# A transformer block on one core: chunks of 256/512/512/512/256 tokens, paired PSUM banks dealt by the scheduler, a separate home for parked sums, and the softmax's maximum taken and subtracted in PSUM

## The chip, the cores and the metric

The kernel runs on one core of a Trainium2 chip. The metric is the device time of one execution in microseconds (us). All executions compared here are in the fast state; of all runs of this study one (of the halved-evictions experiment) fell in the slow state, and it is left out of its verdict.

The engines are called PE (TensorE, matmuls), PEld (its weight loads), DVE (VectorE), ACT (ScalarE), POOL (GpSimd) and SP (SyncE, which issues most transfers). Each engine works through its own queue in the order in which the kernel emits its instructions (the run with statistics on ACT, below, shows what that can cost: DVE waits 6.32 us for an eviction that stands behind other work), so that order is part of the design. "Bank" is one of the 8 parts, each 512 fp32 columns wide, into which the kernel divides PSUM; the matrix unit's results land there, and ACT or DVE carries them out ("eviction").

## The reference, cut to what matters

```python
# x: 2048 tokens x 512, bf16; 32 heads of 16; F = 1792
mod = silu(c) @ w_mod                      # six vectors of 512: sa, ca, ga, sb, cb, gb
h = layernorm(x) * (1 + ca) + sa           # first layernorm, affine from c
q, k, v = split(h @ wqkv)                  # 1536 columns
logits = einsum(q, k at s, s-2, ..., s-14) / 4     # 8 keys per query, 2 apart
attn = softmax(logits)                     # over those 8
x = x + ga * ((attn . v at s, s-2, ...) @ wo)
h = layernorm(x) * (1 + cb) + sb           # second
h = layernorm(h)                           # third
u = gelu(h^T @ w1 + b1)                    # mixes over the 2048 tokens: 512 x 1792
x = x + gb * (u @ w2 + b2)^T
```

The first MLP product sums over tokens. It can therefore be computed in levels: a level adds the tokens that are ready, and the sums are "parked" in between.

## The kernel before

The kernel builds a list of operations with their dependences and estimated durations, and a small list scheduler in Python fixes the order per engine (and, where an operation may run on ACT or DVE, the engine). It works on 4 chunks of 512 tokens. The parts that matter:

```python
# PSUM: fixed roles for the 8 banks
psA = [psp.tile([P, 512], F32, name=f"psA{i}") for i in range(2)]
psL = psp.tile([P, 2, 512], F32, name="psL")          # logits, 8 windows x 128
psT, psX, psO, psW = ...                              # one bank each
# home of the projection weights, later of the parked sums (same memory)
w_raw = wg[:, 0:KT * 3 * D]...;  gT = wg[:]...
...
# start: w_mod through ACT's queue (1 MB), wqkv in one load (1.5 MB);
# columns sa and 1+ca by 32 one-column matmuls; then
#   bqkv = sa @ wqkv                       (48 one-column matmuls, PE)
#   w_raw *= (1 + ca)                      (4 operations, DVE)
...
# softmax of a chunk, after the logits lie in psL
copy2(lsb[b], psL, ...)                               # eviction
m4 = max(lsb[0:4], lsb[4:8]); m2 = ...; m1 = ...      # DVE
lsb = lsb - m1                                        # DVE
ee = exp(lsb)                                         # ACT
s4 = ee[0:4] + ee[4:8]; s2 = ...; s1 = ...            # DVE
rb = reciprocal(s1); ee = ee * rb                     # DVE
...
# layernorm statistics: bn_stats + bn_aggr on DVE, or two summing
# activations and three small ones on ACT, as the scheduler picks
# second MLP product: 16 tiles of 128 tokens, banks psA[0], psA[1] in turn
```

Of the kernel before, what the change touches and what calls it, by code (L numbers as in the profile page):

```python
# [13 lines left out]
P = 128  # L14
# [9 lines left out]
class _Op:  # L24
    __slots__ = ("idx", "alts", "eng", "dur", "lat", "fn", "name", "deps", "succ", "start", "end", "bytes_", "pk")
# [7 lines left out]

class _Graph:
    XLAT = 0.3
    EBIAS = {}
# [3 lines left out]
    def __init__(self):  # L40
        self.ops = []
        self.last_writer = {}
        self.readers = {}
        self.pk = 0.0

    def add(self, eng, dur, fn, reads=(), writes=(), name="", lat=0.0, after=(), bytes_=0, pk=None):
        return self.add_any([(eng, dur, fn)], reads, writes, name, lat, after, bytes_, pk)

    def add_any(self, alts, reads=(), writes=(), name="", lat=0.0, after=(), bytes_=0, pk=None):
        op = _Op(len(self.ops), list(alts), lat, name, bytes_, self.pk if pk is None else pk)  # L50
        deps = set(a.idx for a in after if a is not None)
        for k in reads:
            w = self.last_writer.get(k)
            if w is not None:
                deps.add(w)
        for k in writes:
            w = self.last_writer.get(k)
            if w is not None:
                deps.add(w)
            deps.update(self.readers.get(k, ()))  # L60
        for k in reads:
            self.readers.setdefault(k, []).append(op.idx)
        for k in writes:
            self.last_writer[k] = op.idx
            self.readers[k] = []
        deps.discard(op.idx)
        op.deps = deps
        self.ops.append(op)
        return op

    def schedule(self):
# [7 lines left out]
        avail = set(o.idx for o in ops if not o.deps)  # L79
        order = []  # L80

        def ready_time(o, e):
            r = 0.0
            for d in o.deps:
                od = ops[d]
                t = od.end + (0.0 if od.eng == e else self.XLAT)
                if t > r:
                    r = t
            return r

        while avail:
            per_eng = {}
            for i in avail:
                o = ops[i]
                fin = [(max(ready_time(o, e), eng_free.get(e, 0.0)) + d, e, d) for (e, d, _) in o.alts]
                best_fin = min(f_ + self.EBIAS.get(e, 0.0) for f_, e, d in fin)
                for f_, e, d in fin:
                    if f_ + self.EBIAS.get(e, 0.0) <= best_fin + 0.05:
# [13 lines left out]
            o.start = r  # L112
            if o.bytes_:
# [3 lines left out]
            else:  # L117
                o.end = r + o.dur + o.lat
            eng_free[e] = r + o.dur
# [53 lines left out]
def _t_tt2(n):  # L173
    return 0.15 + 0.00051 * n
# [6 lines left out]
def _t_ts(n):  # L181
    return 0.12 + 0.00043 * n


def _t_act(n, aps=0):
    return 0.12 + 0.00095 * n + 0.06 * aps
# [7 lines left out]
def kernel(  # L194
# [13 lines left out]
    C: int = 512,  # L208
    ORDER: int = 1,
    DUMP: int = 0,  # L210
    RK=(10, 20, 30, 40, 50),
    MK: int = 1000,
    WIN: int = 25,
    LEVELS=(2, 3),
    PARK: int = 0,
    FLEX: int = 1,
    DBIAS: int = 100,
    XLAT: int = 30,
):
    nc = _OrderedNC(tc, ORDER)  # L220
    G = _Graph()
    G.WIN = WIN / 100.0
    G.EBIAS = {"dve": DBIAS / 100.0}
    G.XLAT = XLAT / 100.0
    SB = C // 4
    NCH = S // C
    TPC = C // P
    WPM = min(NW, 512 // SB)
    NHALF = NW // WPM

    x_flat = A_x[0]
    out_flat = out[0]
    x_view = x_flat.rearrange("(t p) d -> p t d", p=P)
    w1_view = B_w1.rearrange("(t p) f -> p t f", p=P)
    w2_view = B_w2.rearrange("(t p) s -> p t s", p=P)
    wmod_view = w_mod.rearrange("(kt p) n -> p kt n", p=P)
    wo_view = A_wo.rearrange("(h q l) n -> l h q n", h=H, q=4, l=4)
# [7 lines left out]
    psA = [psp.tile([P, 512], F32, name=f"psA{i}") for i in range(2)]  # L245
    psL = psp.tile([P, 2, 512], F32, name="psL")
    psT = psp.tile([P, 512], F32, name="psT")
    psX = psp.tile([P, 512], F32, name="psX")
    psO = psp.tile([P, 512], F32, name="psO")
    psW = psp.tile([P, 512], F32, name="psW")  # L250
    psM = [psT, psX, psO]
    NA = 2
    ctrA = [0]

    def nextA():
        ctrA[0] += 1
        return (ctrA[0] - 1) % NA

    xx = T([P, NST, D], BF, "xx")
    wg = T([P, NFT * D], BF, "wg")  # L260
    w_raw = wg[:, 0:KT * 3 * D].rearrange("p (k n) -> p k n", k=KT)
    gT = wg[:].rearrange("p (f d) -> p f d", f=NFT)
    woq = T([P, 4, D], BF, "woq")
    h3 = T([P, NST, D], BF, "h3")
    NB2 = 2
    n_sb = [T([P, TPC, D], BF, "n_sb0")] * NB2
    hT = [T([P, KT, C], BF, f"hT{i}") for i in range(NB2)]
    q_sb = [T([P, 4, C], BF, f"q_sb{i}") for i in range(NB2)]
    k_c = [T([P, 4, PAD + C], BF, f"k_c{i}") for i in range(NB2)]
    v_c = [T([P, 4, PAD + C], BF, f"v_c{i}") for i in range(NB2)]  # L270
    NPROD = 2
    prod = [T([P, 4, NW, SB], BF, f"prod{i}") for i in range(NPROD)]
    lsb = [T([P, NW, SB], BF, f"lsb{i}") for i in range(NB2)]
    ee = [T([P, NW, SB], BF, f"ee{i}") for i in range(NB2)]
    a2sb = [T([P, 2, C], BF, f"a2sb{i}") for i in range(NB2)]
    m4 = T([P, 4, SB], BF, "m4")
    m2 = T([P, 2, SB], BF, "m2")
    m1 = T([P, SB], BF, "m1")
    s4 = T([P, 4, SB], BF, "s4")
    s2 = T([P, 2, SB], F32, "s2")  # L280
    s1 = T([P, SB], F32, "s1")
    rb = T([P, SB], BF, "rb")
    NVD = 3
    vD = [T([P, 8, C + 8], BF, f"vD{i}") for i in range(NVD)]
    NPV = 4
    pv = [T([P, 4, C], BF, f"pv{i}") for i in range(NPV)]
    o_sb = [T([P, 4, C], BF, f"o_sb{i}") for i in range(NB2)]
    h2 = [T([P, TPC, D], BF, f"h2{i}") for i in range(NB2)]
    junk = T([P, D], BF, "junk")
    NWS = 3  # L290
    wst = [T([P, NFT, 256], BF, f"wst{i}") for i in range(NWS)]
    ostage = [h2[i][:].rearrange("p a d -> p (a d)")[:, 2 * D:3 * D] for i in range(2)]
    otmp = [h2[i][:].rearrange("p a d -> p (a d)")[:, 0:2 * D].bitcast(F32) for i in range(2)]
# [7 lines left out]
    sac_bf = T([P, KT], BF, "sac_bf")  # L301
    bqkv = T([P, 12], F32, "bqkv")
# [12 lines left out]
    st6 = [T([P, TPC, 6], F32, f"st6_{i}") for i in range(2)]  # L315
    mv = [T([P, TPC, 2], F32, f"mv{i}") for i in range(2)]
    lv1 = [T([P, TPC], F32, f"lv1_{i}") for i in range(2)]
    rs1 = [T([P, TPC], F32, f"rs1_{i}") for i in range(2)]
    sums = [T([P, TPC, 2], F32, f"sums{i}") for i in range(2)]
    sums1 = [T([P, TPC, 2], F32, f"sums1_{i}") for i in range(2)]  # L320
    sums3 = [T([P, TPC, 2], F32, f"sums3_{i}") for i in range(2)]
    nb1 = [T([P, TPC], F32, f"nb1_{i}") for i in range(2)]
    st6b = [T([P, TPC, 6], F32, f"st6b_{i}") for i in range(2)]
    mv2 = [T([P, TPC, 2], F32, f"mv2_{i}") for i in range(2)]
    lv2 = [T([P, TPC], F32, f"lv2_{i}") for i in range(2)]
    rs2 = [T([P, TPC], F32, f"rs2_{i}") for i in range(2)]
    nb2 = [T([P, TPC], F32, f"nb2_{i}") for i in range(2)]
    st6c = [T([P, TPC, 6], F32, f"st6c_{i}") for i in range(2)]
    mv3 = [T([P, TPC, 2], F32, f"mv3_{i}") for i in range(2)]
    lv3 = [T([P, TPC], F32, f"lv3_{i}") for i in range(2)]  # L330
    rs3 = [T([P, TPC], F32, f"rs3_{i}") for i in range(2)]
    nb3 = [T([P, TPC], F32, f"nb3_{i}") for i in range(2)]
# [3 lines left out]
    def copy2(dst, src_fn, n, bf16_src, reads, writes, name, scale=None):  # L336
        def fa():
            if scale is None:
                nc.scalar.activation(dst, src_fn(), ACT.Identity)
            else:  # L340
                nc.scalar.activation(dst, src_fn(), ACT.Identity, scale=scale)

        def fd():
            if scale is None:
                nc.vector.tensor_copy(dst, src_fn())
            else:
                nc.vector.tensor_scalar(dst, src_fn(), scale, None, op0=ALU.mult)
        alts = [("act", _t_act(n), fa)]
        if FLEX:
            alts.append(("dve", (0.12 + 0.00052 * n) if bf16_src else _t_tt1(n), fd))  # L350
        return G.add_any(alts, reads=reads, writes=writes, name=name)

    def dma(out_ap, in_ap, nbytes, reads, writes, name):
        return add("sp", 0.65, lambda: nc.sync.dma_start(out_ap, in_ap), reads=reads, writes=writes, name=name,
                   bytes_=nbytes)

    def ln_stats(src_fn, evac_dst, st6_ap, mv_ap, sums_ap, reads, writes, name):
        def fd():
            x = src_fn()
            if evac_dst is not None:  # L360
                nc.vector.tensor_copy(evac_dst, x)
                x = evac_dst
            nc.vector.bn_stats(st6_ap, x)
# [504 lines left out]
```

## Time and profile before

The kernel before took 254.2 us (median of 3 runs, 253.66 to 254.49); the profiled execution had a span of 251.4 us.

| Stretch (us) | What happens | What limits it |
|---|---|---|
| 0 to 17.6 | loads, first layernorm, columns from c, weight scaling | waits on loads |
| 20 to 120 | most of the attention of the four chunks | DVE |
| 147 to 194 | most of the first MLP product | PE |
| 198.7 to 247.2 | second MLP product, 16 groups of 14 matmuls | PE |
| 247.2 to 251.4 | last eviction and store | tail |

First, lines of the page of the kernel before: the busy time of each engine with its share of the span, then the span in 40 equal slices, each digit the busy share in tenths; "PEclk" is the granted TensorE clock in tenths.

```profile
span 251.4 us, 3545 instructions
...
PE 209.5 (83%) x1295; PEld 91.2 (36%) x1295; DVE 166.0 (66%) x238; ACT 152.3 (61%) x343; POOL 7.8 (3%) x32
...
PE   0188994998989236996789989999899999999993
...
DVE  3169999899999998799955998214900044444443
...
PEclk9999997799999755697999999999999999999999
...
```

PE is busy most of the time, but not all: in the 14th and 15th slice (a slice is 6.3 us, so 82 to 94 us) its row drops to 2 and 3 while the DVE row stays at 9, and the clock row falls with it. The next lines are from the table of busy time by windows of the kernel before (window, its length, then each engine's busy time with the number of its instructions, the granted clock, the share and rate of the transfers).

```profile
...
core 0: us, PE busy (x) PEld busy (x) DVE busy (x) ACT busy (x) POOL busy (x), PEclk, DMA share, GB/s
20.00:40.00 20.00, 16.45 (x103) 7.22 (x102) 19.19 (x30) 14.48 (x32) 1.49 (x9) 1.00 0.42 112
40.00:60.00 20.00, 18.11 (x136) 7.24 (x135) 18.91 (x19) 14.75 (x24) 1.90 (x2) 0.83 0.82 134
60.00:80.00 20.00, 18.69 (x151) 8.29 (x151) 19.63 (x22) 16.04 (x36) 0.67 (x1) 1.00 0.68 105
80.00:100.00 20.00, 9.24 (x60) 2.89 (x59) 19.29 (x33) 17.60 (x42) 0.89 (x1) 0.62 0.66 90
100.00:120.00 20.00, 17.36 (x116) 7.21 (x116) 17.05 (x18) 15.81 (x39) 0.00 (x0) 0.78 0.14 18
...
```

DVE is busy 19.19, 18.91, 19.63 and 19.29 of 20 us up to 100 us, PE only 9.24 of 20 in the last of them. DVE is the bottleneck of this stage. PE stands idle for 10.8 us of the last window; the list of its waits puts about half of that down to DVE (5.3 us) and half to ACT (5.6 us), mostly to ACT's late evictions of the one bank psO. The start is read from the timeline of PE in the kernel before (start, duration, operation, and in brackets the idle time before it with what ended it):

```profile
...
2.21 0.18 PE L144 MATMUL psT<-ident,c_t 4*128 4x4 bf16 x1 [2.21 <-DMA c_t<-in_c_dram]
11.79 0.40 PE L144 MATMUL psO<-ident,b_t 14*128 14x14 bf16 x2 [9.39 <-DMA b_t<-in_B_b_dram]
12.12 1.01 PE L144 MATMUL psX<-sc,vD_96 128*128 128x1 bf16 x32
...
17.63 2.33 PE L144 MATMUL psA_61<-hT_73,wg 128*128 128x512 bf16 x4
...
```

PE idles 9.39 us and the profile puts the wait down to a bias load. Finally, the softmax on DVE, from the groups of instructions of the kernel before (operation, tiles, shapes, count, then busy time in us, mean ns of one, and the idle time before):

```profile
...
L144 DVE RECIPROCAL rb<-s_94 128x128 bf16<-128x128 f32 x4 | 3.8, 952 | 0.1
...
L144 DVE TENSOR_TENSOR lsb_84<-lsb_84,m_91 128x1024 bf16<-128x1024 bf16 x2 | 1.4, 693 | 0.1
L144 DVE TENSOR_TENSOR ee_85<-ee_85,rb 128x1024 bf16<-128x1024 bf16 x2 | 1.4, 692 | 0.1
...
L144 DVE TENSOR_TENSOR m_89<-lsb_84 128x512 bf16<-128x512 bf16 x2 | 0.8, 418 | 2.8 <-ACT lsb_84 L144 2.8
...
```

One reciprocal of 128 columns costs 952 ns, the subtraction and the scaling 692 ns each. The first step of the maximum tree had waited 2.8 us for ACT to copy the logits out of PSUM.

### The profile page before, as it was taken

Reading aid. Unit: us, or ns where it says so; the run is one execution under the profiler, and the core shown is the slowest. Engines: PE = TensorE matmul, PEld = TensorE weight load, DVE = VectorE, ACT = ScalarE, POOL = GpSimd, SP = SyncE. Lnnn points to the kernel's source line nnn. Section 1 sums busy time; section 2 is a strip of 40 time slices with the busy share of each in tenths; the row PEclk is TensorE's granted clock in tenths of the full one; section 3 lists DMA queues with packets and bytes.
Section 4 is the critical chain, followed back from the end, with each engine's and each line's share of the span. In section 5 each row is a group of like instructions: output and inputs, shape, how many; then the busy total and the mean of one; then the engine's idle time right before and its main releaser. Section 6 shows DMA issues by size and latency. Waiting matters only on the chain.

```text
span 251.4 us, 3545 instructions
## 1 busy us (share of the span) xinstructions
PE 209.5 (83%) x1295; PEld 91.2 (36%) x1295; DVE 166.0 (66%) x238; ACT 152.3 (61%) x343; POOL 7.8 (3%) x32
## 2 busy tenths in 40 slices
PE   0188994998989236996789989999899999999993
PEld 0163431433434002432234433444344344444441
DVE  3169999899999998799955998214900044444443
ACT  5178568768886889697997797688786400000000
POOL 4000110011001100000000000000000000000000
PEclk9999997799999755697999999999999999999999
DMA  6995239974880099300009994123424966666311
GB/s 244 385 296 165 83 124 146 149 174 85 147 110 3 0 157 141 45 0 1 0 25 170 151 247 128 43 71 95 128 87 122 319 190 202 206 196 207 104 42 42
DMA packets 46596, 32.87 MB, mean 131 GB/s; under 512 B 2036, under 2 KB 45556, under 8 KB 46580
## 3 DMA queue, kind: packets, MB, share of 16 engines
q1 hardware_dynamic: 45984, 31.60, 53.9%
q10 hardware_dynamic: 596, 1.06, 1.1%
q8 instruction: 10, 0.16, 0.3%
q14 instruction: 6, 0.05, 0.1%
HBM read 22.03 MB, written 2.10 MB: 96 GB/s over the span
## 4 chain that ended last, share of the span: by engine, by line
PE 52%; DVE 18%; ACT 16%; DMA 8%; issue 3%; SPq 2%; ACTq 0%; DVEq 0%
PE psA_61 L144 19%; PE psA_62 L144 19%; PE psW L144 5%; PE psT L144 4%; DMA wst_108<-in_B_w_dram 4%; DMA b_t<-in_B_b_dram 4%; ACT junk L144 3%; DVE h_106 L144 3%; ACT h_71 L144 2%; PE psL L144 2%; ACT h_106 L144 2%; PE psO L144 2%; SPq L144 2%; DVE st6c_158 L144 1%; DVE rb L144 1%
## 5 line engine op out<-in xcount | busy, mean ns | idle before, releaser
L144 PEld LDWEIGHTS <-wg 128*128 128x128 bf16 x240 | 22.9, 118 | 34.1 <-issue 18.8
L144 DVE SCALAR_TENSOR_TENSOR h_105<-psA_61,b2col,gb_bc 128x512 f32<-128x512 f32 x8 | 6.0, 751 | 30.0 <-PE psA_61 L144 30.0
L144 PEld LDWEIGHTS <-wst_108 128*128 128x128 bf16 x164 | 15.9, 98 | 21.3 <-DMA wst_108<-in_B_w_dram 2.4
L144 PEld LDWEIGHTS <-wst_109 128*128 128x128 bf16 x156 | 15.0, 98 | 19.9 <-issue 2.2
L144 PE MATMUL psA_61<-hT_74,wg 128*128 128x512 bf16 x48 | 15.0, 437 | 3.8 <-DVE k_c_78 L144 1.9
L144 PEld LDWEIGHTS <-wst_110 128*128 128x128 bf16 x128 | 12.4, 98 | 15.3 <-issue 0.4
L144 PE MATMUL psA_62<-hT_74,wg 128*128 128x512 bf16 x48 | 14.0, 419 | 2.5 <-ACT q_sb_76 L144 1.5
L144 ACT ACTIVATE junk<-xx 128x512 bf16<-128x512 bf16 x23 | 14.5, 629 | 0.6
L144 PE MATMUL psA_61<-hT_73,wg 128*128 128x512 bf16 x48 | 13.7, 401 | 1.1 <-ACT k_c_77 L144 1.0
L144 DVE SCALAR_TENSOR_TENSOR h_106<-psA_62,b2col,gb_bc 128x512 f32<-128x512 f32 x8 | 6.0, 751 | 12.4 <-PE psA_62 L144 12.4
L144 ACT ACTIVATE xx<-psW 128x512 bf16<-128x512 f32 x15 | 9.0, 598 | 6.9 <-PE psW L144 6.7
L144 PE MATMUL psA_62<-hT_73,wg 128*128 128x512 bf16 x48 | 12.5, 384 | 0.0
L144 PE MATMUL psW<-woq,o_sb_104 128*128 128x512 bf16 x32 | 10.7, 461 | 0.3 <-ACT o_sb_104 L144 0.3
L144 PE MATMUL psA_61<-h_71,wst_108 128*128 128x512 bf16 x40 | 9.8, 379 | 0.8 <-DMA wst_108<-in_B_w_dram 0.8
L144 DVE CAST wg<-psA_61 128x512 bf16<-128x512 f32 x4 | 2.8, 692 | 11.5 <-PE psA_61 L144 11.4
L144 PE MATMUL psO<-pv_101,stack_113 128*32 128x512 bf16 x32 | 3.6, 443 | 8.0 <-ACT o_sb_104 L144 4.6
L144 PE MATMUL psA_61<-wg,wst_108 128*128 128x512 bf16 x42 | 9.6, 379 | 0.6 <-DMA wst_108<-in_B_w_dram 0.6
L144 PE MATMUL psT<-ident,n_sb_72 128*128 128x128 bf16 x64 | 6.8, 265 | 3.8 <-ACT hT_74 L144 2.5
L144 PE MATMUL psA_62<-h_71,wst_108 128*128 128x512 bf16 x40 | 9.8, 379 | 0.0
L144 DVE TENSOR_TENSOR prod_81<-q_sb_76,k_c_78 128x4096 bf16<-128x4096 bf16 x4 | 9.2, 2288 | 0.9 <-ACT q_sb_76 L144 0.9
L144 PE MATMUL psA_62<-wg,wst_108 128*128 128x512 bf16 x42 | 9.6, 379 | 0.0
L144 PE MATMUL psA_61<-wg,wst_109 128*128 128x512 bf16 x42 | 9.6, 379 | 0.0
(211 smaller groups left out, 442.5 us busy)
## 6 DMA issues: line engine op xcount, KB each, us to landing
wst_108<-in_B_w_dram SPq DMA_DIRECT2D x3, 896.0 KB, 4.8
wst_109<-in_B_w_dram SPq DMA_DIRECT2D x3, 896.0 KB, 4.8
vD_97<-v_c_79 SPq DMA_DIRECT2D x16, 130.0 KB, 5.5
vD_96<-v_c_80 SPq DMA_DIRECT2D x16, 130.0 KB, 4.5
xx<-in_A_x_dram SPq DMA_DIRECT2D x4, 512.0 KB, 10.9
wst_110<-in_B_w_dram SPq DMA_DIRECT2D x2, 896.0 KB
wg<-in_A_wqkv_dram SPq DMA_DIRECT2D x1, 1536.0 KB, 9.4
wst_108<-in_B_w_dram SPq DMA_DIRECT2D x3, 512.0 KB, 6.3
```

The costliest lines, as they stand in the source:

```text
L144: r = fn(*a, **k)
```

## The change

Its intent: take work off DVE and off the start, let PE start MLP work as soon as tokens are ready, and use the PSUM banks more freely. The diff, cut to its core (`...` marks cuts; the scheduler's cost figures and its bookkeeping of banks are left out):

```diff
-    C: int = 512, ...  LEVELS=(2, 3),
+    SIZES=(2, 4, 4, 4, 2),  LEVELS=(2, 3, 4),     # in tiles of 128 tokens
...
-    psA = [... for i in range(2)];  psT, psX, psO, psW = one bank each
+    psG = [psp.tile([P, 1024], F32, name=f"psG{i}") for i in range(3)]
+    def ps(slot):                 # slot.i is picked by the scheduler
+        lo = slot.i % 2 * 512
+        return psG[slot.i // 2][:, lo:lo + slot.size * 512]
...
-    w_raw = wg[:, 0:KT * 3 * D]...;  gT = wg[:]...
+    w_raw_t = T([P, KT * 3 * D], BF, "w_raw")     # later a home for w2
+    gT = T([P, NFT, D], BF, "gT")
...
+    # x of the first chunk in two tiles, w_mod in two parts, w_raw in three
+    for t in (1, 0, 2): dma(w_raw[:, :, t*D:(t+1)*D], ...)
-    bqkv = sa @ wqkv;  w_raw *= (1 + ca)
+    # the affine rides on the eviction of the transposes
+    nc.vector.tensor_scalar(hT[:, kt, :], src(), a1col, sacol, mult, add)  # or ACT
...
-    lsb = copy(psL); m4, m2, m1 = max tree; lsb -= m1; ee = exp(lsb)
-    s4, s2, s1 = sum tree; rb = reciprocal(s1); ee *= rb
+    nc.vector.tensor_reduce(m1, psL, XY, max)                   # DVE, from PSUM
+    matmul(psL, lhsT=-identity, rhs=m1, start=False)            # PE subtracts
+    nc.scalar.activation(ee, psL, Exp, scale=DH ** -0.5)        # ACT, from PSUM
+    for w in range(8): matmul(ps(s_s), lhsT=identity, rhs=ee[:, w])   # PE sums
+    rb = exp(-ln(sum))                                          # ACT
+    ee *= rb                                                    # DVE, as before
...
-    layernorm statistics on DVE or ACT, as the scheduler picks
+    layernorm statistics on DVE (but for two tiles of the second
+    layernorm in chunks 2 to 4, which ACT sums while evicting)
...
-    evictions of 512 columns
+    evictions of 1024 columns, two banks at a time, where a pair is free
+    # the last tile of the second MLP product in two halves of 256 columns
```

## The prediction

> **What bounds it now.** The page: span 251.4 us (time 254.2, 2.8 us more); PE busy 83%, DVE 66%, ACT 61%. By stretches (busy table over windows):
> - 0 to 17.6 us, start: PE idles 9.4 us for the bias loads (waits), because a bias matmul stands first in PE's order. First projection matmul at 17.6 us, steady from 22 us.
> - 20 to 120 us, attention: DVE is busy 90 to 100% in most 10 us windows. PE depends on it: 4.7 and 4.5 of 10 us busy in 80 to 100, granted clock 0.75 and 0.50 there.
> - 147 to 194 us, first MLP product, and 198.7 to 247.2, second: PE saturated. The second is 16 groups of 14 matmuls at 3.02 us (chain of waits), 216 ns each. The Trainium skill (TensorE: Matmul & The Clock Gate, Back-to-back issue gap) gives 512/2.4 + 2.5 = 216 ns; the trace agrees.
> - Tail 4.2 us.
>
> **What changes.**
> - Start: bias loads leave PE's way; two 128 KB x tiles and split weight loads come first; scaling the projection weight (2.2 us DVE), its bias product (1.8 us PE) and the 9.4 us wait go, the affine rides on the transposes' eviction. Projections should start near 9 us: about -9.
> - DVE: softmax max, subtract and sum trees plus reciprocal (about 4 us a chunk, times 4) become a max reduce from PSUM, about 1.2 us by estimate (the skill, VectorE: DVE Perf Modes, Side-by-side, counts one element a cycle; the 692 ns of a 512-wide PSUM copy fits). But all first and third and part of the second layernorm statistics go to DVE: 42 pairs of 0.80 us against 25. Summing the instruction list with the trace's durations, DVE before the final stage stays about 139 us (143 before).
> - ACT: pairs of banks halve the evictions (1.01 us for 1024 columns against 2 x 0.59); statistics leave. Sum about 132 us against 152.
> - PE: +14 parking reads (3.0 us), +negated-max products (2) and exp sums (2.5), -bias products. Sum about 201 us, 5 more.
> - Own parking home, more homes for the second weights: PE idled only 0.6 us there, so little. Halved last tile: about -1.
>
> **Critical path.** In PE's new order no MLP matmul stands before the fourth chunk's logits. DVE has 84.5 us of work up to there. With 5 us done by 14 us, the rest at 93% busy (20 to 120 us of before: 93%) ends near 99 us. From there PE has about 126 us: 106 MLP, 20 attention remainder. DVE needs 54 us more, which the MLP covers. So 99 + 126, + 3 stalls, + 3 tail, + 2.8 = 234; I shade it to 231 since ACT is lighter and may let DVE reach 95%.
>
> **Prediction: 231 us, range 222 to 241; faster by over 2%: 0.95, within 2%: 0.03, slower: 0.02.**
>
> **Right if** the profile shows the first projection matmul by 10 us, DVE at or above 93% from 14 to 99 us, the first MLP matmul at 95 to 103 us, PE idle under 4 us from there to the last matmul, second product again 48.4 us, DVE before the final stage 135 to 143 us, ACT 125 to 140.
>
> **Wrong if** six paired banks make PE wait on ACT evictions in attention; the PSUM reduce or the 4096-wide product over overlapping reads is slower than assumed; the serial chain max, subtract, exp, sum, log, exp stalls DVE; PE loses clock before 99 us; or DVE's idle gaps vanish (under 222).

## The result

The changed kernel took 238.31 us (median of 4 runs, 238.14 to 238.81) beside 253.93 us (251.75 to 254.49, 4 runs) for the kernel before. The ratio is 0.942, with a 95% interval from 0.937 to 0.947. Ratios, here and below, are worked out from the fast runs of both kernels in the same rounds, and so are not quite the ratio of the medians quoted. It is 15.6 us faster. The output was correct.

The same rows of the page of the changed kernel:

```profile
span 236.5 us, 3678 instructions
...
PE 206.4 (87%) x1413; PEld 100.6 (43%) x1436; DVE 157.8 (67%) x231; ACT 129.4 (55%) x209; POOL 3.7 (2%) x29
...
PE   0493678899988995889999999999999999999992
...
DVE  4207979997999979989969987662600044444445
...
PEclk9999599999999999999999999999999999999998
...
```

and its table by windows:

```profile
...
core 0: us, PE busy (x) PEld busy (x) DVE busy (x) ACT busy (x) POOL busy (x), PEclk, DMA share, GB/s
20.00:40.00 20.00, 12.64 (x106) 6.75 (x108) 17.61 (x38) 12.34 (x23) 0.00 (x0) 0.83 0.63 182
40.00:60.00 20.00, 19.00 (x146) 9.00 (x147) 18.69 (x23) 13.45 (x22) 0.00 (x0) 1.00 0.65 141
60.00:80.00 20.00, 17.67 (x157) 8.31 (x159) 19.81 (x18) 17.63 (x27) 0.00 (x0) 1.00 0.83 118
80.00:100.00 20.00, 17.12 (x130) 9.53 (x131) 18.36 (x26) 16.09 (x32) 0.00 (x0) 1.00 0.35 63
100.00:120.00 20.00, 18.58 (x184) 8.91 (x186) 17.69 (x13) 14.16 (x23) 0.00 (x0) 1.00 0.75 164
...
```

In 80 to 100 us PE is now busy 17.12 of 20 us instead of 9.24, at a granted clock of 1.00 instead of 0.62. DVE is still busy 18.36 there, so it still sets the pace, but each chunk needs less of it. Over the whole kernel DVE's busy time fell from 166.0 to 157.8 us and ACT's from 152.3 to 129.4. The start, in the timeline of PE in the changed kernel:

```profile
...
10.55 0.37 PE L188 MATMUL psG_63<-hT_71,w_raw 128*128 128x256 bf16 x1 [2.20 <-DMA w_raw<-in_A_wqkv_dram]
11.96 3.39 PE L188 MATMUL psG_63<-hT_71,w_raw 128*128 128x256 bf16 x15 [1.04 <-DMA w_raw<-in_A_wqkv_dram]
15.14 2.67 PE L188 MATMUL psG_61<-hT_71,w_raw 128*128 128x256 bf16 x16
17.65 1.91 PE L188 MATMUL psG_62<-hT_71,w_raw 128*128 128x256 bf16 x16
...
```

The first projection matmul starts at 10.55 us instead of 17.63, but the next one waits again for the weight load, and the 15 matmuls after that take 3.39 us where the 16 of the group at 17.65 take 1.91 us. DVE in the same stretch of the changed kernel:

```profile
...
9.31 0.73 DVE L188 TENSOR_SCALAR hT_71<-psG_62,a1col,sacol 128x256 bf16<-128x256 bf16 x2 [0.69 <-ACT hT_71 L188]
18.96 1.23 DVE L188 TENSOR_TENSOR big_78<-q_sb_72,k_c_74 128x2048 bf16<-128x2048 bf16 x1 [8.93 <-issue]
20.10 0.69 DVE L188 BATCH_NORM_STATS2 st_0_1_123<-xx 128x6 f32<-128x512 bf16 x1
...
23.31 1.19 DVE L188 TENSOR_TENSOR big_79<-q_sb_72,k_c_74 128x2048 bf16<-128x2048 bf16 x1
...
```

DVE gets its first query-key product ("big" from q and k) at 18.96 us, after 8.93 us of idling. The profile calls the cause "issue", but ACT's eviction of q ends at 18.87 us in the same trace, just ahead of it. Behind that first product DVE runs the four statistics pairs of the second chunk, from 20.10 us to the product at 23.31 us; while DVE stood idle these lay behind the product in its queue. Where the PE-bound part begins, in PE's timeline of the changed kernel:

```profile
...
104.21 1.02 PE L188 MATMUL psG_61<-h_69,wst_98 128*128 128x512 bf16 x3 [1.00 <-ACT a2sb_83 L188]
...
```

The first matmul of the MLP ("h" times "wst") comes at 104.21 us. From there to PE's last matmul, which ends at 232.2 us, PE is busy 126.7 of 128.0 us. In the kernel before, the first MLP matmul came at 130.35 us, and from there to the last PE was busy 114.4 of 116.8 us. So the MLP starts 26.1 us earlier, and 11.2 us of that are given back because PE has more work left at that point; the difference, 14.9 us, is that of the two profiled spans. The new maximum, from the groups of the changed kernel:

```profile
...
L188 DVE TENSOR_REDUCE m_87<-psL 128x128 bf16<-128x1024 f32 x3 | 3.6, 1212 | 0.8 <-PE psL L188 0.8
...
```

And the end, in the timeline of DVE in the changed kernel:

```profile
...
226.19 0.75 DVE L188 SCALAR_TENSOR_TENSOR o_sb_95<-psG_62,b2col,gb_bc 128x512 f32<-128x512 f32 x1 [3.18 <-PE psG_62 L188]
...
227.58 0.74 DVE L188 SCALAR_TENSOR_TENSOR o_sb_95<-psG_62,b2col,gb_bc 128x512 f32<-128x512 f32 x1
...
230.74 0.75 DVE L188 SCALAR_TENSOR_TENSOR o_sb_95<-psG_61,b2col,gb_bc 128x512 f32<-128x512 f32 x1 [1.69 <-PE psG_61 L188]
...
```

The evictions of the second product come in twos: one waits 3.18 us for PE, the next follows at once. In the kernel before, there was one per 3.02 us, each after a wait of 1.54 us, as in this line of its DVE timeline:

```profile
...
241.19 0.75 DVE L144 SCALAR_TENSOR_TENSOR h_106<-psA_62,b2col,gb_bc 128x512 f32<-128x512 f32 x1 [1.54 <-PE psA_62 L144]
...
```

The tail after the last matmul is 4.3 us in the changed kernel and was 4.2.

### The profile page after: what moved, and what is told of

Read it like the earlier page. It is cut to its first block, busy times and chain, and to the rows that moved or that the text cites. A ratio compares the mean times of both kernels' runs of the same rounds, so it can differ in the third digit from the quotient of the medians.

```text
span 236.5 us, 3678 instructions
## 1 busy us (share of the span) xinstructions
PE 206.4 (87%) x1413; PEld 100.6 (43%) x1436; DVE 157.8 (67%) x231; ACT 129.4 (55%) x209; POOL 3.7 (2%) x29
## 4 chain that ended last, share of the span: by engine, by line
PE 58%; DVE 17%; ACT 11%; issue 7%; DMA 4%; SPq 1%; DVEq 0%; ACTq 0%
PE psG_61 L188 21%; PE psG_62 L188 21%; PE psG_63 L188 15%; ACT xx L188 3%; DMA w_raw<-in_A_wqkv_dram 3%; DVE big_78 L188 2%; DVE big_79 L188 2%; DVE st_0_1_123 L188 2%; DVE big_80 L188 2%; ACT junk L188 2%; ACT h_69 L188 2%; PE psL L188 1%; DMA vD_93<-v_c_77 1%; SPq L188 1%; DVE st_2_1_143 L188 1%
## 5 line engine op out<-in xcount | busy, mean ns | idle before, releaser
L188 PEld LDWEIGHTS <-w_raw 128*128 128x128 bf16 x282 | 30.8, 114 | 28.1 <-issue 7.6
L188 DVE SCALAR_TENSOR_TENSOR o_sb_95<-psG_62,b2col,gb_bc 128x512 f32<-128x512 f32 x6 | 4.5, 748 | 24.6 <-PE psG_62 L188 24.6
L188 PEld LDWEIGHTS <-wst_99 128*128 128x128 bf16 x128 | 12.2, 98 | 15.6 <-issue 1.8
L188 PE MATMUL psG_61<-hT_71,w_raw 128*128 128x512 bf16 (+1 forms) x78 | 17.8, 372 | 0.9 <-DVE ga_bc L188 0.5
L188 PE MATMUL psG_62<-hT_71,w_raw 128*128 128x256 bf16 (+1 forms) x95 | 17.7, 327 | 0.5 <-ACT hT_71 L188 0.4
L188 PE MATMUL psG_63<-hT_71,w_raw 128*128 128x256 bf16 (+1 forms) x62 | 13.0, 360 | 3.3 <-DMA w_raw<-in_A_wqkv_dram 3.2
L188 DVE TENSOR_TENSOR big_78<-q_sb_72,k_c_74 128x2048 bf16<-128x2048 bf16 (+1 forms) x5 | 8.2, 1646 | 8.9 <-issue 8.9
L188 PEld LDWEIGHTS <-ident 128*128 128x128 bf16 (+1 forms) x99 | 7.9, 97 | 12.4 <-issue 5.6
L188 DVE TENSOR_TENSOR n_sb<-o_sb_95,xx 128x512 bf16<-128x512 f32 (+1 forms) x17 | 11.2, 660 | 0.6
L188 PE MATMUL psG_62<-h_69,wst_99 128*128 128x512 bf16 x40 | 10.8, 379 | 0.5 <-issue 0.3
L188 ACT ACTIVATE gT<-psG_62 128x1024 bf16<-128x1024 f32 x9 | 9.2, 1017 | 3.4 <-PE psG_62 L188 3.4
L188 PE MATMUL psG_63<-h_69,wst_99 128*128 128x512 bf16 x39 | 10.7, 380 | 0.1
L188 DVE SCALAR_TENSOR_TENSOR o_sb_95<-psG_61,b2col,gb_bc 128x512 f32<-128x512 f32 (+1 forms) x6 | 4.2, 703 | 8.0 <-PE psG_61 L188 8.0
L188 PE MATMUL psG_62<-h_69,wst_100 128*128 128x512 bf16 x35 | 8.9, 380 | 0.1
L188 ACT ACTIVATE gT<-psG_63 128x1024 bf16<-128x1024 f32 x7 | 7.1, 1016 | 2.7 <-PE psG_63 L188 2.7
L188 DVE SCALAR_TENSOR_TENSOR o_sb_95<-psG_63,b2col,gb_bc 128x512 f32<-128x512 f32 (+1 forms) x5 | 3.5, 693 | 6.3 <-PE psG_63 L188 6.3
## 6 DMA issues: line engine op xcount, KB each, us to landing
out_dram<-n_sb SPq DMA_DIRECT2D x15, 128.0 KB, 1.7
```

The costliest lines, as they stand in the source:

```text
L188: r = fn(*a, **k)
```

## The experiments

Two kinds of edit must be told apart in a kernel whose order is computed. If a part is undone and the scheduler runs again, it may choose another order everywhere. If the operations keep their places in the computed order and only what they do is exchanged, that part alone is measured. The names of runs say which it is where it matters. All outputs were correct. The kernel before, run on the same chip beside each batch, had medians of 252.7 to 253.5 us.

### Undo the softmax in PSUM, scheduler free

```diff
-    tensor_reduce from psL; subtract and sum on PE; exp(-ln) on ACT
+    copy2(ee, psL); max tree; subtract; exp; sum tree; reciprocal; multiply
```

> The changed kernel with its old softmax put back (logits evicted to SBUF, max tree, subtract, exp, sum tree, reciprocal on DVE). Theory A, DVE sets the pace until the first MLP matmul (104.2 us in the changed kernel) and PE after it: DVE gains about 2.6 us per full chunk, so about 7 us of it before that matmul; the first MLP matmul moves to about 111 us and the time to 244 to 247 us, although PE loses about 4 us of work. Theory B, PE or ACT latencies set the pace: the time stays within 2 us of 238 or falls.

It took 258.54 us, ratio 1.019 [1.012, 1.025]: 20 us slower than the changed kernel, slower even than the kernel before. The first MLP matmul came at 113.4 us, and PE idled another 7.05 us, up to 153.1 us, for DVE. The edit also let the scheduler deal a new order, so the cause was not yet separated. The expectation (244 to 247 us) was missed by more than 11 us: the first MLP matmul came 2.4 us later than it said, and after it PE was idle for 11.1 of 139.6 us, where the changed kernel is idle for 1.3 of 128.0.

### The same, order kept

```diff
     add("dve", ..., f, name=f"max{ch}")    # f: copy (ACT), max tree, subtract
-    add("pe", ..., subtract, name=f"sub{ch}")
+    add("pe", ..., lambda: None, name=f"sub{ch}")        # place kept
-    rb = exp(-ln(sum on PE))
+    sum tree and reciprocal on DVE, at the same place
```

> The changed kernel with the old softmax work put inside the same nodes, so that the scheduler gives every other instruction the same place; the free run of the scheduler (e1) took 258.5 us with its first MLP matmul at 113.4. Theory A, DVE pace: first MLP matmul at 111 to 114 us, then again about 128 us to the last matmul, time 244 to 248 us; the rest of e1 was then the scheduler's other order. Rival: the serial chain of the old softmax itself costs it: 254 us or more here too.

It took 252.55 us, ratio 0.997 [0.993, 1.002], so the change without this part gains nothing. The softmax in PSUM is worth 0.055 of 253.5 us, or 14 us, within the rest of the change. DVE's busy time was 168.2 us, 10.4 more than in the changed kernel; its maximum trees also waited 5.0 us for ACT's copy of the logits. PE's timeline of this run, from its first MLP matmul on:

```profile
...
113.79 2.32 PE L188 MATMUL psG<-h,wst 128*128 128x512 bf16 x10 [1.02 <-ACT a2sb L188]
118.67 0.62 PE L188 MATMUL psG<-big,stack 128*32 128x512 bf16 x8 [2.56 <-DVE big L188]
...
125.12 0.62 PE L188 MATMUL psG<-big,stack 128*32 128x512 bf16 x8 [2.24 <-DVE big L188]
...
```

The first MLP matmul came 9.6 us later. From there to its last matmul PE was busy for the same 126.7 us, but in 133.2 us instead of 128.0: it idled 6.5 us, 5.0 of them for DVE's products of the attention that was left. So the old softmax costs 9.6 us before the first MLP matmul and 5.2 us after it. Theory A had counted with 128 us after it again, which is why its 244 to 248 us were missed; the rival's 254 us were not reached either. The other 6 us of the run with the scheduler free came with its other order.

### Equal chunks of 512

```diff
-    SIZES=(2, 4, 4, 4, 2), LEVELS=(2, 3, 4), LN2A=(0, 2, 2, 2, 0)
+    SIZES=(4, 4, 4, 4),    LEVELS=(2, 3),    LN2A=(2, 2, 2, 0)
```

> The changed kernel with four chunks of 512 tokens and three MLP levels. Theory A: the first logits product waits for a projection twice as wide, and the first MLP level needs 8 tiles instead of 6, so DVE and PE both start later; PE saves 14 parking reads (3 us). Expect 241 to 246 us. Rival: the split buys nothing, because the 3 us of parking reads pay for the earlier start: 236 to 239 us.

It took 244.51 us, ratio 0.965 [0.959, 0.971], some 6 us slower than the changed kernel. The number is that of theory A, but its reason is not: PE starts MLP work at 100.2 us, 4.0 us earlier than in the changed kernel and not later. It then runs out of it, as a line of its table by windows shows:

```profile
...
100.00:120.00 20.00, 6.68 (x94) 2.82 (x94) 18.47 (x25) 10.88 (x20) 0.00 (x0) 0.70 0.31 68
...
```

In 100 to 120 us PE is busy 6.68 of 20 us while DVE works through the last chunk's attention. That a short last chunk shortens this stretch fits, but is not shown apart: the edit changes the first chunk, the levels and the free order with it, so the 6 us are those of all these together.

### One bank at a time, scheduler free; and halved evictions, order kept

```diff
# e3_single_banks
-    PR = dict(tr=1, qkv=2, a2=2, o=2, wo=2, mlp=2)
+    PR = dict(tr=1, qkv=1, a2=1, o=1, wo=1, mlp=1)
# e3b_halved_same_order: an eviction of 1024 columns on ACT becomes
+    activation(dst[:, 0:h, :], s[:, 0:h, :]); activation(dst[:, h:, :], s[:, h:, :])
```

> The changed kernel with every paired eviction made single (64 evictions of 1024 columns become 128 of 512). ACT gains roughly 10 us of busy time (129 to about 140). Theory A, ACT is not what binds: 237 to 240 us. Rival, halved evictions are a main source of the gain: 243 us or more.

> The changed kernel, same order and banks, each 1024-wide eviction issued as two of 512. ACT busy rises from 129 to about 140 us. If evictions do not bind (theory A): 238 to 240 us, and the 249.3 us of single banks (e3) came from the other order. If they bind: 245 us or more.

With single banks it took 249.35 us (ratio 0.986 [0.979, 0.993]), 11 us slower. With the evictions halved in place it took 237.88 us (0.944 [0.938, 0.951], one slow run left out), the same as the changed kernel, although ACT's busy time rose from 129.4 to 132.6 us. So the 11 us of the single-bank run do not come from the evictions' own cost. The test is a small one, though: 61 evictions more made ACT busy for only 3.2 us more, some 0.05 us each and not the 10 us expected, and halving also hands over the first half earlier (the first query-key product began at 17.76 us, before the eviction of q was done at 18.16 us). What pairing is worth lies in the order: in the single-bank run PE is busy 14.26 of 20 us in 60 to 80 us (changed kernel: 17.67), and the first MLP matmul came at 109.1 us. Which of the scheduler's choices did that was not followed up.

### Parked sums back in the projection weights' memory

```diff
-    w_raw_t = T([P, KT * 3 * D], ...);  gT = T([P, NFT, D], ...)
+    w_raw_t = T([P, NFT * D], ...);     gT = w_raw_t[:]...
```

> The changed kernel with the parked sums again in the projection weights' buffer, and that buffer no longer a home for second-product weights. The first MLP matmul stands after the last projection in PE's order anyway, so theory A expects 237.5 to 239 us, no change. Rival, the parking or the prefetch of the second weights waits: 241 us or more, with PE idle at the first MLP matmuls or at the step to the second product.

It took 238.91 us, ratio 0.942 [0.937, 0.947]: no change, as expected. The separate home buys nothing by itself.

### The kernel before, bias matmuls moved back

```diff
+    bias = [o for o in order if o.name in ("biascols", "biascols_cp")]
+    order = rest up to and including w_scale + bias + rest
```

> The kernel before, with the bias matmuls and their two copies moved behind the scaling of the projection weight; nothing else moves. Theory A (as in the prediction): the 9.4 us wait of PE on the bias loads is what delays the start, so the first projection matmul comes many us before 17.6 and the time falls by 6 us or more. Rival: the 1 MB modulation load, behind which nothing can be done, also lands only at about 12 us, so the bias wait hid it: the first projection matmul at 16 to 17 us and the time 0 to 2 us less.

It took 250.35 us, ratio 0.991 [0.987, 0.995], a gain of 2.4 us and not 9; of the two theories the rival (0 to 2 us) came nearest. PE's timeline of this run, at the start:

```profile
...
11.56 1.01 PE L144 MATMUL psX<-sc,vD 128*128 128x1 bf16 x32 [9.18 <-DMA vD<-in_w_mod_dram]
...
15.97 3.38 PE L144 MATMUL psA<-hT,wg 128*128 128x512 bf16 x8
```

With the bias matmuls out of the way PE waits 9.18 us for the load of w_mod ("vD" is the memory that it lies in). The bias had been only the last of several to arrive. A wait belongs to the last event; taking that event away leaves the one before it.

### Statistics of the second chunk ahead of the first query-key product

```diff
+    stats = [o for o in order if o.name in ("ln1s2", "ln1s3", "ln1s4", "ln1s5")]
+    order = rest up to the first qk0_ operation + stats + rest
```

> The changed kernel with the four statistics pairs of the second chunk ahead of the first logits product in DVE's queue, where DVE stood idle for 8.9 us. They are 3.2 us of DVE work. Theory A: the first MLP matmul at 101 us and the time 3 us less (235 to 236). Rival, the start is bound by PE's projections and the gain is absorbed by other waits: less than 1 us.

It took 235.6 us, ratio 0.932 [0.928, 0.935], 2.7 us faster than the changed kernel. The first MLP matmul came at 101.96 us, 2.3 earlier. These are the four pairs that DVE could have done while it idled before 18.96 us. In this run it does them from 14.41 us on. The first product starts when it did before (18.94 us), and the second follows it at once, so that PE waits for it 0.74 us (3.91 us in the changed kernel), as PE's timeline of this run shows:

```profile
...
21.36 0.40 PE L188 MATMUL psL<-big,group 128*32 128x512 bf16 x4 [0.74 <-DVE big L188]
...
```

### Keep PE busy while it waits for its first weights

```diff
+    def warm(n):      # dummy products into the half of psL that is not yet used
+        for i in range(n): matmul(psL[:, 1, :], lhsT=ident, rhs=xx[:, 0, :])
     # warm(5) after the first matmul, warm(6) after the columns from c
```

> Changed kernel with 11 dummy 512-wide matmuls on TensorE while it waits for the first weights, order otherwise the same. Theory (the first 16 projection matmuls ran at 213 ns each because TensorE had been idle): the k group takes 1.9 to 2.2 us instead of 3.18 and the q group 1.9 instead of 2.51, q is evicted 1 to 2 us earlier, the first MLP matmul comes at 102.5 to 103.5 us instead of 104.2, and the time falls by 1 to 2 us to 236.5 to 237.3 (ratio to before 0.932 to 0.937). Rival (the landing of the weights and the order on VectorE govern, not the pace of TensorE): the groups get faster but the first MLP matmul stays at 104 and the time within 0.5 us of the changed kernel.

It took 236.63 us, ratio 0.935 [0.931, 0.939], 1.7 us faster. PE's timeline of this run:

```profile
...
12.78 5.32 PE L188 MATMUL psG<-hT,w_raw 128*128 128x256 bf16 x47 [1.15 <-DMA w_raw<-in_A_wqkv_dram]
18.78 0.40 PE L188 MATMUL psL<-big,group 128*32 128x512 bf16 x4 [0.68 <-DVE big L188]
...
```

The 47 projection matmuls after the first take 5.32 us, 113 ns each; in the changed kernel they ran from 11.96 to 19.56 us. The first reduction of products follows at 18.78 us (20.24 there), and the first MLP matmul at 102.50 us. The theory's numbers held. The size is less certain than the direction: the interval of the ratio overlaps that of the changed kernel (0.937 to 0.947). DVE's first query-key product, which sets the pace from here, began at 17.50 us, and at 18.42 to 19.32 us in the profiles of five runs whose start is the changed kernel's, so the warm start is worth some 1 to 2 us.

### Banks of the second product dealt apart

```diff
     s_ = _Slot("ps")
+    s_.want = (0, 2, 4, 1, 3, 5)[(st + hh) % 6]    # neighbours in different pairs
```

> Changed kernel with the banks of the second product's tiles dealt in the order 0, 2, 4, 1, 3, 5, so that two groups in succession never lie in the same pair of banks; order identical. Theory (each pair is one tile to the dependence tracking, so the eviction of a bank waits for the matmul group in the other bank of its pair): the waits of 3.18 us of VectorE on TensorE in the second product go, VectorE's last evictions no longer come in twos, and the end comes 0.9 us earlier (237.3). Rival (the last group alone sets the tail): no change within 0.4 us.

It took 238.85 us, ratio 0.943 [0.940, 0.947]: no gain. The trace tells why. A line of PE's timeline at the join of the two products, and the last of DVE's evictions, of this run:

```profile
...
184.93 9.22 PE L190 MATMUL psG<-gT,w_raw 128*128 128x512 bf16 x41 [0.40 <-ACT gT L190]
...
```

```profile
...
230.45 0.75 DVE L190 SCALAR_TENSOR_TENSOR o_sb<-psG,b2col,gb_bc 128x512 f32<-128x512 f32 x1 [1.55 <-PE psG L190]
...
233.51 0.48 DVE L190 SCALAR_TENSOR_TENSOR o_sb<-psG,b2col,gb_bc 128x256 f32<-128x256 f32 x1 [0.59 <-PE psG L190]
...
```

The waits of 3.18 us are gone, each eviction now follows 1.54 us after the one before is done, and the tail after PE's last matmul is 3.6 us instead of 4.3. That half of the theory held: a pair is one tile to whoever tracks the dependences, so reading one bank waits for the group in the other. But the fixed deal made the second product begin on a bank that a gelu still occupied, which cost PE 0.40 us; with it, the way from the first MLP matmul to the last matmul's end took 128.6 us instead of 128.0. The profiled run also started its MLP 0.7 us later (104.90), with the same program up to there; its 47 first matmuls, cold (that is, slow after PE had been idle), took 8.19 us.

### The three together, and statistics on ACT

```diff
# g1_all_three: the three edits above
# g2_stats_on_act: g1, and for the fourth chunk's first layernorm
-    bn_stats, bn_aggr (DVE, 4 tiles)
+    activation(junk, src, Identity, accum_out=...)   # ACT, at the same places
+    activation(junk, src, Square, scale=D ** -0.5, accum_out=...)
```

> The two edits of this batch (warm TensorE, banks apart) and the one of the batch before (second chunk's statistics ahead of the first query-key product), together. If their gains add: 2.7 + 1 to 2 + 0.9, so 233 to 234.5 us, ratio 0.920 to 0.926. If warming and the reordering of statistics remove the same wait of VectorE: 234.5 to 235.5.

> The combination, and the fourth chunk's first-layernorm statistics moved from VectorE (2.75 us less) to ScalarE (5.7 us more, ahead of the first MLP matmul). Theory (VectorE paces the stretch up to the first MLP matmul): the first MLP matmul comes some 2 us earlier than in the combination and the time falls by 2 us, to 231.5 to 233. Rival (ScalarE works in order, so its evictions come late and TensorE or VectorE then waits on them): same as the combination within 0.7 us, or slower, with more idle time of VectorE put down to ScalarE.

The three together took 234.84 us (232.88 to 236.17, 6 runs), ratio 0.925 [0.921, 0.930]: 7.5% below the kernel before, and the best kernel by its median and ratio (its interval overlaps that of the statistics edit alone). The first MLP matmul came at 100.58 us, 3.6 us earlier than in the changed kernel, where the two start edits alone had given 2.3 and 1.7. In time the gain over the changed kernel is 3.5 us, where the two had given 2.7 and 1.7. The median lies in the range that was expected if the two edits remove in part the same wait (234.5 to 235.5 us), and the interval (233.4 to 235.7 us) reaches into both ranges; so whether the gains add is not settled.

Moving more statistics to ACT gave 239.84 us, ratio 0.945 [0.941, 0.948], 5 us slower than the combination, although DVE's busy time fell by 2.5 us. Its timelines, of ACT and of DVE:

```profile
...
36.63 0.62 ACT L190 ACTIVATE junk<-xx 128x512 bf16<-128x512 bf16 x1
...
37.37 0.63 ACT L190 ACTIVATE junk<-xx 128x512 bf16<-128x512 bf16 x1
...
38.00 0.58 ACT L190 ACTIVATE a2sb<-psG 128x512 bf16<-128x512 f32 x1
...
```

```profile
...
38.61 3.50 DVE L190 TENSOR_TENSOR big<-a2sb,vD 128x2048 bf16<-128x2048 bf16 x3 [6.32 <-ACT a2sb L190]
```

ACT works in order. It sums statistics of a chunk that nobody needs yet, and the eviction of the attention weights ("a2sb") comes behind them at 38.00 us; DVE idles 6.32 us for it. In the combination the same product begins at 35.06 us and does not wait. The first MLP matmul came at 104.59 us. The rival explanation held. This does not show that ACT cannot take that work, only that it cannot take it at these places in its queue: the order was kept from the combination, which had planned the work for DVE.

## Why the prediction was right or wrong, point by point

The prediction of 231 us was 7 us low: of a gain of 23 us, 15.6 came. Its direction was right with a large margin, and its range (222 to 241) was wide enough to hold the result. Its unshaded sum was 234 us. Of the signs that it named, three were missed by a little: the first projection matmul (10.55 us, not by 10), DVE's busy share from 14 to 99 us (87.7%, not 93%) and the first MLP matmul (104.21 us, not by 103). All three hang on the start.

- **DVE paces the stretch up to the MLP: right.** DVE's work between 20.2 us and the first MLP matmul took 84.0 us, of which DVE was busy 77.7 (92.5%). The prediction had 79.5 us of work left at 93%. The softmax run with the order kept, the statistics run and the warm run each moved the first MLP matmul (by 9.6, 2.3 and 1.7 us), and the end moved by as much or more (14, 2.7 and 1.7 us).
- **The softmax: right in mechanism and size.** The estimate for the maximum from PSUM was 1.2 us, and the trace has 1212 ns for 1024 columns. The Trainium skill (VectorE: DVE Perf Modes, Side-by-side) counts one element a cycle plus a fixed part in its 1x mode, which works out at about 1.23 us for 1024 (an estimate from that section). Predicted was a saving of 2.8 us a chunk on DVE, 11.2 in all; DVE had 10.4 us more busy time with the old softmax in place. In time it is worth more, 14 us: with the old softmax DVE also waits for ACT's copy of the logits (5.0 us), and PE still waits for DVE after the first MLP matmul.
- **The start, -9 us: this is the step that failed.** In the words of the prediction, "Projections should start near 9 us: about -9" and DVE has "5 us done by 14 us". The first projection matmul came at 10.55 us, 7.1 us earlier than before, but DVE had that 5 us of work done only at 20.2 us: the first query-key product moved from 23.08 to 18.96 us, 4.1 us. So the term of the sum was mis-sized by 6.2 us. Three things made it up. The bias load was not what the start hung on: moving it alone gained 2.4 us, and the load of w_mod stood right behind it. PE's first matmuls ran at half speed (1.7 us by the warm run). And DVE's queue held work it could have done behind a product that was not ready (2.7 us by the statistics run). The rest, some 2 us, is what is left over: it is put down to the landing of the weights, at 10 to 13 us in the profiles of the changed kernel and its variants, but no run tested that.
- **99 us for the first MLP matmul: late by 5.2, at 104.21,** just outside the 95 to 103 named. The start's 6.2 us, less 1 us for slightly less work than counted.
- **126 us of PE and 3 us of stalls: right.** It was 128.0 us, with 1.3 us idle. The second product took 48.5 us, as before. Its 14 matmuls of 512 columns take 3.02 us, 216 ns each, as the Trainium skill gives (TensorE: Matmul & The Clock Gate, Back-to-back issue gap, the formula for the warm clock, there for an isolated matmul).
- **The tail, 3 us: too low by 1.3.** "Halved last tile: about -1" failed, as the banks were dealt in pairs: DVE's eviction of the last whole tile waited for the first half tile in the other bank of its pair, and was in the way when the last half was done. With banks apart the tail is 3.6 us.
- **The 3 us of shading, for ACT being lighter: wrong.** DVE's busy share in its stretch stayed at 92.5%. That ACT's lower load as a whole (129.4 us against 152.3) is worth nothing is not shown: the halved evictions gave back only 3.2 us of it, without loss, and the run with statistics on ACT shows that ACT can hold DVE up.
- **DVE before the final stage 135 to 143 us, ACT 125 to 140:** 135.2 (157.8 less 22.65 in the last stretch) and 129.4; both held, DVE at the low end. "Own parking home ... little" held too.

In sum: 234 + 6.2 (start) - 1.0 (DVE's work) - 1.0 (PE's stretch) + 1.3 (tail) - 1.0 (the time outside the span was 1.8 us, not 2.8) = 238.5 us, against 238.3 measured. Errors of +7.5 and -3.0 us cancelled in part, which is luck.

What stays open: which choices of the scheduler make the single-bank version 11 us slower and the free-order softmax run 6 us slower than the one with the order kept, and how far the start could fall if w_mod and the weights landed earlier. The change also gave the scheduler new cost figures and priorities; no run tests these alone.

## What to carry to other kernels

A wait in a profile names the last event only; before counting it as gain, look for the event that would have come next, and if it can be tried, move the named one alone. In a kernel whose order a scheduler computes, test a part with the order kept as well as with the scheduler free: here the two answers differed by 6 and by 11 us. And look at what stands behind an idle engine in its own queue, for moving ready work ahead of a wait was the cheapest gain here, while adding work to an engine with idle time made things worse as soon as it stood ahead of an eviction.

## What the Trainium skill lacked or had wrong

- TensorE: Matmul & The Clock Gate (Part 1) describes the cold clock and says that its length varies from run to run; this case agrees (15 matmuls of 256 columns at about 212 ns each after a wait, which is 256/1.2; 47 of them took from 6.6 to 8.2 us in the profiles where PE's program is the same up to there, and 5.3 us warm). It puts the penalty under 1% of a typical kernel and advises against fitting a count of cold matmuls; the 1.7 of 238.3 us (0.7%) that 11 dummy matmuls in idle time gained here agree with that, and were still worth an edit, as the bottleneck hung on the cold ones. The granted-clock row of the profile read 1.00 in that stretch, so it does not show it; the page warns that clock records can be unreliable, but does not name this case.
- The same page, Back-to-back issue gap, gives about 131 ns as the sustained spacing of 512-column matmuls in a stream of weight loads and matmuls, and 216 ns for an isolated one. Sustained over 16 groups of 14 with a weight load each, this case has 216 ns, so the 131 ns do not hold here.
- VectorE: DVE Perf Modes (First, the fixed hardware budget) says how a reciprocal runs but gives no duration: here it took 952 ns for 128 columns (kernel before) and 553 ns for 64 (old softmax, order kept). The logarithm and the exponential on ScalarE that replace it took 274 and 310 ns for 128.
- PSUM — Partial Sum Buffer (PSUM bank collisions raise a hardware error) advises to guard PSUM by bank and quadrant, or simply by bank, but has nothing on what it costs when a tile of two banks is guarded as one: an eviction from one bank waited 3.18 us, until the group in the other was done, and 1.54 us with neighbouring groups in different pairs.
